# A gated Fourier and window-attention kernel: early loads at its start, another deal of its last projections

## The chip, the cores and the metric

The kernel runs on one core of one Trainium2 chip. The metric is the device time of one execution in microseconds. The engines are called as the profile calls them: PE (TensorE, matrix products) with PEld (its weight loads), DVE (VectorE), ACT (ScalarE), POOL (GpSimd) and SP (SyncE, which issues nearly all transfers here).

## The reference

The input x has 2048 tokens of width 512. Two mixers run on it and a gate mixes them.

```python
x = A_x                                                   # 1 x 2048 x 512
g = sigmoid((x * gate_w).sum(-1, keepdims=True))
# A: Fourier mixing, real part of a transform over width and tokens
a  = einsum("bsd,ed->bse", x, dft_hid_re)
b  = einsum("bsd,ed->bse", x, dft_hid_im)
A  = einsum("ts,bse->bte", dft_seq_re, a) - einsum("ts,bse->bte", dft_seq_im, b)
# B: causal attention in a window of 256 tokens, 32 heads of width 16
q, k, v = split(x @ wqkv)                                 # wqkv: 512 x 1536
scores  = q @ k.T / 4, kept where 0 <= i - j < 256
B       = (softmax(scores) @ v) @ wo                      # wo: 512 x 512
return g * A + (1 - g) * B
```

## The kernel before, in words

Every product of 32-bit data is made of three matmuls on rounded halves (`TERMS`): an operand is split into a rounded part `hi` and a rest `lo` (`split`, lines 76 to 81: a cast, then a subtract on DVE at L81; the cast is on ACT at L78 or on DVE at L80). A 512-column product over 512 inputs is thus 12 matmuls.

There are two strands of work. The attention strand walks over n = 0 to 147: 128 steps of scores (4 head groups times 32 blocks of 64 queries, `s_pair`, L363), and, 19 steps behind (`LAG`), the transposed scores, their exponent and the products with v (`t_pair` L445, `pv` L471). Before a step's scores its heads are laid into zero-padded tiles (`make_pad`, L344 and L346, which multiply by the 0/1 column `half`). Per eight steps (index u) the row maxima and sums are split, turned by PE and copied out (`ml_split`, `ml_turn` at L383, `ml_rows`), and loaded as extra rows of the keys (`m_ring`), so that the transposed scores hold them; the table `TURN` says at which step each of these comes.

The other strand is `dense()`, a generator that gives one matmul at a time: projections to q and k (L277) and to v and the transform over the width (both L300), then the transform over tokens, output block by output block (16 blocks of 128 tokens; 16 chunks of three matmuls for each half, L523). `fill` takes a set number of its matmuls between the steps of attention. When attention is over, the rest of `dense()` runs alone: that is called the tail here.

PE's order is the order of the program text. The other engines and SP's queue are ordered by hand only in the first block of the text; after that a scheduler orders them, held where the text says so: `mark` and `behind` pin instructions of an engine behind the last marked one, and `late` does so for the work that it is given. SP's queue issues in order: a transfer that waits for its data holds those behind it.

Start: the first quarter (block 0) of x transposed is loaded into buffers of the pool `pt`, which holds attention's exponents later and has four buffers. The other three blocks go through the pool `raw`, which has two buffers and also carries wv and the other weights: `load_x` loads two of the four 128-row pieces of a block, `x_job` splits one and asks for the next load.

Rows 96 to 99 of the second pair of padded tiles hold ones and zeros that meet the maxima's rows: `clear_pads` writes ones with GpSimd and multiplies by the column `mrow` on DVE (L214).

Tail: o, the attention's output, is normalised on DVE (L492) and stored in four quarters to `o_scr`. For each block of 128 tokens, `wo_prep` loads it back turned, in pieces of 512 bytes (`fin<-o_scr`), and splits it (ACT L78, DVE L81; tile `os`), and `wo_block` multiplies it by wo in 12 matmuls (L793) and adds its share to a part that lies in `r_scr` (L795). A transform's block goes to `r_scr` by `add_r` (L735), or straight to the output, if the projection of its block is there already (`mixed`). The loop over `tb` makes, between two blocks of the transform (48 matmuls each), all the output projections that were prepared at the block before, 8 of them together; the last block (`c_final`) ends the kernel with its last two chunks apart (L550).

Of the kernel before, what the change touches and what calls it, by code (L numbers as in the profile page):

```python
# [14 lines left out]
P = 128  # L15
# [4 lines left out]
NP = 4  # L20
# [12 lines left out]
def fnet_window_mix(ctx: ExitStack, tc: tile.TileContext, xT, x, wqk, wv, wr, wi, cr, ci, wo, gw, out):  # L33
# [21 lines left out]
    def ld(dst, src):  # L55
        mark("sp", nc.sync.dma_start(dst, src))  # L56

    def f(ap):
        return ap.bitcast(F32)
# [4 lines left out]
    def mark(e, ins):  # L64
        last[e] = ins.ins
# [10 lines left out]
    def split(hi, lo, raw, act=False):  # L76
        if act:
            nc.scalar.copy(hi, raw)  # L78
        else:
            nc.vector.tensor_copy(hi, raw)  # L80
        nc.vector.tensor_sub(lo, raw, f(hi))  # L81

    def split_psum(hi, lo, ps, scale=1.0):
        mark("act", nc.scalar.activation(hi, ps, AF.Copy, scale=scale))
# [7 lines left out]
    def load_raw(src):  # L92
        raw = st.tile([P, 1024], F32, name="raw", bufs=2)
        ld(raw, src)
        return raw
# [29 lines left out]
    XRAW = {}  # L125

    def load_x(ss, j):
        raw = st.tile([P, 1024], F32, name="raw", bufs=2)
        ld(raw.rearrange("p (k s) -> p k s", k=2), xT[ss, 2 * j:2 * j + 2].rearrange("k p s -> p k s"))
        for c in range(2):  # L130
            XRAW[2 * j + c, ss] = raw[:, HALVES[c]]

    def split_x(ss, dks, act=False):
        for dk in dks:
            XT[dk, ss] = big.tile([P, 2, 512], F32R, name="big")
            split(XT[dk, ss][:, 0], XT[dk, ss][:, 1], XRAW.pop((dk, ss)), act)


    def pt_raw():
# [36 lines left out]
    nc.gpsimd.affine_select(ident[:], f(ident[:]), pattern=[[1, P]], compare_op=OP.is_equal, fill=0.0,  # L176
                            base=0, channel_multiplier=-1)

    cols = const.tile([P, 4], F32, name="half")
    half, side = cols[:, :2], cols[:, 2:]  # L180
    mrow = const.tile([P, 2], F32, name="mrow")
    for t, edges in ((half, ((0, 16, 32, 48, 64, 80), (16, 32, 48, 64, 80, 96))), (mrow, ((96, 98), (98, 100)))):
        nc.gpsimd.memset(t, 0.0)
        for h in range(2):
            for i, e in enumerate(edges[h]):
                a = t[:, h:h + 1]
                nc.gpsimd.affine_select(a, a, pattern=[[0, 1]], compare_op=OP.is_ge, fill=1.0 - i % 2,
                                        base=e - 1, channel_multiplier=-1)

    nc.vector.reduce_sum(side[:, 0:1], f(ident[:]).rearrange("p (r h) -> p h r", h=2)[:, 0],  # L190
                         axis=mybir.AxisListType.X)
# [17 lines left out]
    def clear_pads():  # L209
        for t in pads[1]:  # L210
            nc.gpsimd.memset(f(t[96:128]), 1.0)
            for h in range(2):
                a = turned(t)[96:128, :, :, h]
                nc.vector.tensor_scalar(a, f(a), mrow[96:128, h:h + 1], None, op0=OP.mult)  # L214


    gl = const.tile([P, 16], F32, name="gl")
# [301 lines left out]

    def c_part(w, chunks, ab, ps, ends):  # L520
        for i in chunks:
            for n, (a, b) in enumerate(TERMS):
                nc.tensor.matmul(ps, w[a][:, i % 8 * 128:i % 8 * 128 + 128], ab[SC[i]][:, b],  # L523
                                 start=i == ends[0] and a + b == 0, stop=i == ends[1] and a == 1)
                job(i % 8 * 3 + n + 1)
                if i != chunks[-1] or a == 0:
                    yield

    def c_block(get, half, tb, ab, done):
        ps = ps_d.tile([P, 512], F32, name="dc", tag="d")  # L530
        for j in range(2):
            yield from c_part(get((half, tb * 2 + j)), range(16)[8 * j:8 * j + 8], ab, ps, (0, 15))
            if j == 0:
                yield
        ended.append(lambda: late(done, tb, ps))
        yield

    def c_final(get, ab, r):
        ps = ps_d.tile([P, 512], F32, name="dc", tag="d")
        g = g1[:, 15:16]  # L540
        for j in range(2):
            w = get((1, 30 + j))
            yield from c_part(w, range(16)[8 * j:8 * j + 8 - 2 * j], ab, ps, (0, 13))
            yield
        late(nc.vector.scalar_tensor_tensor, r, ps, g, r, OP.mult, OP.add)
        for c, dma in ((slice(0, 256), nc.sync), (slice(256, 512), nc.scalar)):
            ps2 = ps_a.tile([P, 512], F32, name="t", tag="st")
            for i in (14, 15):
                for a, b in TERMS:
                    nc.tensor.matmul(ps2[:, c], w[a][:, i % 8 * 128:i % 8 * 128 + 128], ab[SC[i]][:, b, c],  # L550
                                     start=i == 14 and a + b == 0, stop=i == 15 and a == 1)
            nc.vector.scalar_tensor_tensor(r[:, c], ps2[:, c], g, r[:, c], op0=OP.mult, op1=OP.add)
            dma.dma_start(out[15][:, c], r[:, c])
        yield
# [22 lines left out]
    def late(fn, *args):  # L577
        with behind("act", "dve"):
            return fn(*args)  # L579
# [6 lines left out]
    def dense():  # L586
        warm()
        with behind("sp"):
            wraw = [load_raw(wv[i]) for i in range(2)]
        wvs = [late(split_raw, r, True) for r in wraw]  # L590
        qk_first(wq0)
        load_x(1, 0)
        load_x(1, 1)
        yield
        def x_job(ss, dk):
            late(split_x, ss, (dk,), ss == 1)
            if dk % 2 and ss < 3:
                load_x(ss + 1, dk // 2)

        for ss in range(4):  # L600
            if ss < 3:
# [117 lines left out]
                                  add(lambda t: r_scr[0][t], lambda t: r_scr[2][t]),  # L719
                                  next_b if j else None, tb + 1 if j and tb < 15 else None)  # L720
        ab = nxt
        wait = []

        mixed = {}

        def r_in(tb):
            return r_scr[2 if tb in lasts else 0][tb]
# [15 lines left out]
                                  add(lambda t: r_scr[2][t], lambda t: r_scr[1][t], wait.append),  # L743
                                  None if j else next_b, tb + 1 if tb + 1 < SWITCH else None)
        for tb in range(SWITCH, 16):
            if FIN:
                while ended:
                    ended.pop(0)()
            if tb in O:
                mixed[tb] = wo_block(tb, 0)  # L750
            for w in [w for w in wait if w in O]:
                wait.remove(w)
                ld(out[w], wo_block(w, 1))
            if FIN and tb < 15:
                for w in (tb + 1, *wait[:-(-len(wait) // (15 - tb))]):
                    wo_prep(w)
            yield from c_block(pieces.get, 1, tb, ab, add_r) if tb < 15 else c_final(pieces.get, ab, mixed.pop(15))

    FIN = []

    def attention_done():
        fin = const.tile([P, 8192], F32R, name="fin", tag="ring0")
# [15 lines left out]
    def wo_prep(tb):  # L778
        oraw = ORAW[0]
        ORAW.append(ORAW.pop(0))  # L780
        ld(oraw, o_scr[tb // 4][:, :, tb % 4 * P:tb % 4 * P + P].rearrange("g p t -> p g t"))
        O[tb] = OS[0][:, next(slot) % 8]
        split(O[tb][:, 0], O[tb][:, 1], oraw[:], True)

    def wo_block(tb, half):
        o = O.pop(tb)
        r = ev.tile([P, 512], F32, name="ev")
        ld(r, r_scr[half if half or tb < 16 - SWITCH else 2][tb])
        ps = ps_a.tile([P, 512], F32, name="t", tag="st")
        n = 0  # L790
        for g in range(NG):
            for a, b in TERMS:
                nc.tensor.matmul(ps, o[:, a, g], FIN[0][:, g // 2, g % 2, b], start=n == 0, stop=n == 11)  # L793
                n += 1
        nc.vector.scalar_tensor_tensor(r, ps, g0[:, tb:tb + 1], r, op0=OP.mult, op1=OP.add)  # L795
        return r
# [5 lines left out]
    def need(key):  # L802
        while key not in have:
            next(stream)
# [23 lines left out]
    ctx.enter_context(tc.manual_schedule(engines={mybir.EngineType.PE}))  # L828
    N = NG * NB
    TURN = (8, 1, ml_split), (9, 1, ml_turn), (9, 2, ml_rows), (12, 0, m_ring)  # L830
    need(("qk", 0, 0))
    ring_ahead(0)
    need(("v", 5))
# [10 lines left out]
    for n in range(N + LAG + 1):  # L844
        if n in (1, 3, 5):
            for i in range(2):
                clear_rows(1 - i, (n + 1) // 2)
        if n == 7:
            clear_pads()
        k = n - LAG  # L850
        ring_ahead(n + 1)
        if k in (-1, 4):
            v_spread(0 if k < 0 else 4)
        if k in (-4, -1, 4):
            v_next({-4: 0, -1: 4, 4: 8}[k])
        if n == 0:
            make_pad(0, 0)
        for p in range(NP):
            if n < N:
                s_pair(n, p)  # L860
            fill(n)
            if 0 <= k < N:
                t_pair(k, p)
            if p == 0:
                make_pad(0, n + 1)
                if k >= -1:
                    make_pad(1, k + 1)
            fill(n)
            for at_n, at_p, do in TURN:
                u, j = divmod(n - at_n, 8)  # L870
                if p == at_p and j == 0 and 0 <= u < 16:
                    do(u)
            if p == 3 and k % 8 == 6 and 0 <= k < N:
                l_load(k // 8)
            if p == 0 and full:
                o_out()
            if p == 2 and (k - summed >= (5 if more else 3) or k == N):
                for j in range(summed, k):
                    pv(j)
                summed = k  # L880
            if p == 3 and 4 * spread - 5 < summed and 4 * spread < N and n >= fresh:
                v_spread(4 * spread)
                spread += 1
                v_next(4 * spread)
                fresh = n + 2
# [49 lines left out]
```

## Time and profile before

| | us |
|---|---|
| median of 3 runs | 853.51 (853.19 to 854.07) |
| the profiled execution, time | 854.57 |
| the profiled execution, span | 852.9 |
| PE busy | 844.8 (99%) |
| DVE busy | 615.8 (72%) |
| ACT busy | 593.7 (70%) |
| POOL busy | 251.9 (30%) |
| bytes moved by transfers | 160.99 MB, mean 189 GB/s |

The span runs from the first to the last instruction that the profiler saw; the time of that execution holds a little more around it. In a timeline a row is start, duration, engine, line, operation, output<-inputs, size and count, and in brackets the idle time of the engine before it and what ended that. A `c` in front of a product's name marks the transform over tokens (`dc`), `dqk`, `dv` and `dab` the projections, `s` and `t` the scores and the transposed scores; `t` is also the result of an output projection.

### The profile page before, as it was taken

The numbers are of one execution on the slowest core, as the hardware profiler recorded it, in microseconds if no ns is written. First come the engines' busy times: TensorE is split into PE (matmuls) and PEld (weight loads), VectorE is DVE, ScalarE is ACT, GpSimd is POOL, SyncE is SP. The second block draws the span as 40 slices with busy tenths as digits, with TensorE's granted clock in tenths as the row PEclk, the third lists the DMA queues.
The fourth block names the chain that finished last, engine by engine and source line by source line (L and its number), as shares of the span: only waits on it lengthen the run. The fifth ranks groups of instructions, "written<-read, shape, count | busy, mean of one in ns | idle before, by whom it ended". The sixth has DMA issues, their size and how long they took to land.

```text
span 852.9 us, 16687 instructions
## 1 busy us (share of the span) xinstructions
PE 844.8 (99%) x5166; PEld 691.3 (81%) x5166; DVE 615.8 (72%) x2013; ACT 593.7 (70%) x1793; POOL 251.9 (30%) x585
## 2 busy tenths in 40 slices
PE   9999999999999999999999999999999999999998
PEld 7788788788788888888878887888888887877887
DVE  5588978667878787669777787788888774437531
ACT  5388798878888987779878897778777765532200
POOL 9000222333332333333423324333243354510000
PEclk9999999999999999999999999999999999999999
DMA  7876578576675275444435557989784344359542
GB/s 255 276 235 201 172 247 249 198 236 210 205 249 181 59 210 127 152 125 143 148 120 145 164 144 216 286 278 292 242 225 140 117 153 144 124 176 303 158 147 98
DMA packets 94344, 160.99 MB, mean 189 GB/s; under 512 B 26800, under 2 KB 35760, under 8 KB 94256
## 3 DMA queue, kind: packets, MB, share of 16 engines
q1 hardware_dynamic: 93824, 159.28, 59.8%
q8 instruction: 40, 0.66, 0.3%
q10 hardware_dynamic: 432, 0.66, 0.2%
q14 instruction: 48, 0.39, 0.1%
HBM read 108.27 MB, written 51.64 MB: 187 GB/s over the span
## 4 chain that ended last, share of the span: by engine, by line
PE 92%; DMA 4%; DVE 2%; ACT 1%; issue 1%; SPq 0%; DVEq 0%; ACTq 0%
PE dc L523 39%; PE dab L300 10%; PE s L363 9%; PE t L445 8%; PE o L471 8%; PE dqk L277 8%; PE t L793 5%; PE dv L300 4%; DMA raw<-xT 1%; DMA fin<-o_scr 1%; DMA o_scr<-ev 1%; DVE sm L365 1%; DMA pt<-wqk 0%; DVE big L81 0%; SPq L56 0%
## 5 line engine op out<-in xcount | busy, mean ns | idle before, releaser
L368 ACT ACTIVATE sm<-sm,ml 128x320 f32<-128x320 f32 (+4 forms) x512 | 277.9, 544 | 101.1 <-DVE ml L365 96.4
L523 PE MATMUL dc<-big,hi 128*128 128x512 f32 x1020 | 344.4, 393 | 0.0
L365 DVE CUSTOM_DVE_ANT_0 sm<-s,mask 128x320 f32<-128x320 f32 (+4 forms) x512 | 235.3, 464 | 113.2 <-PE s L363 91.5
L523 PE MATMUL dc<-big,lo 128*128 128x512 f32 x510 | 200.6, 393 | 0.0
L523 PEld LDWEIGHTS dc<-big,hi 128*128 128x128 f32 x1020 | 179.7, 188 | 21.4
L446 ACT ACTIVATE pt<-t 128x320 f32<-128x320 f32 (+4 forms) x392 | 160.3, 411 | 43.0 <-PE t L445 40.9
L450 POOL TENSOR_SCALAR_AFFINE_SELECT pt<-pt 128x128 f32<-128x128 f32 x196 | 72.2, 368 | 302.0 <-ACT pt L446 299.8
L363 PE MATMUL s<-ring,pad 128*128 128x320 f32 (+4 forms) x512 | 157.7, 308 | 0.0
L445 PE MATMUL t<-ring,pad 128*128 128x320 f32 (+4 forms) x512 | 154.1, 301 | 0.1
L346 DVE TENSOR_SCALAR pad<-ring,half 96x256 fp32r<-96x256 f32 x384 | 119.9, 358 | 13.5 <-PE t L445 13.3
L363 PEld LDWEIGHTS s<-ring,pad 128*128 128x128 f32 x512 | 96.1, 188 | 30.3 <-issue 9.0
L445 PEld LDWEIGHTS t<-ring,pad 128*128 128x128 f32 x512 | 96.1, 188 | 22.0 <-DVE ml L365 1.0
L523 PEld LDWEIGHTS dc<-big,lo 128*128 128x128 f32 x510 | 95.9, 188 | 13.8 <-issue 1.6
L368 ACT ACTIVATION_READ_ACCUMULATOR sm<-sm,ml 128x1 f32 x512 | 97.7, 191 | 0.0
L428 POOL TENSOR_SCALAR vpad<-vr,half 128x256 f32<-128x256 f32 x64 | 60.5, 958 | 124.9 <-DMA vr<-v_scr 75.7
L579 DVE TENSOR_TENSOR lo<-raw,hi 128x512 fp32r<-128x512 f32 x142 | 96.8, 691 | 0.1
L300 PE MATMUL dab<-hi,big 128*128 128x512 f32 x256 | 89.2, 394 | 0.0
L277 PE MATMUL dqk<-big,hi 128*128 128x512 f32 x240 | 85.7, 394 | 1.5 <-DVE big L81 0.9
L579 DVE CAST hi<-raw 128x512 fp32r<-128x512 f32 x142 | 60.1, 432 | 18.7 <-PE dc L523 13.0
L344 ACT ACTIVATE pad<-ring,half 96x256 fp32r<-96x256 f32 x128 | 66.6, 520 | 0.0
L454 POOL TENSOR_SCALAR_AFFINE_SELECT pt<-pt 128x128 f32<-128x128 f32 x172 | 62.0, 361 | 0.1
L446 ACT ACTIVATE home<-t 128x320 f32<-128x320 f32 (+4 forms) x120 | 49.0, 408 | 13.4 <-PE t L445 11.5
(97 smaller groups left out, 915.3 us busy)
## 6 DMA issues: line engine op xcount, KB each, us to landing
qk_scr<-home SPq DMA_DIRECT2D x32, 512.0 KB
ring<-qk_scr SPq DMA_DIRECT2D x32, 512.0 KB
raw<-cr SPq DMA_DIRECT2D x32, 512.0 KB
raw<-ci SPq DMA_DIRECT2D x32, 512.0 KB
r_scr<-ev SPq DMA_DIRECT2D x42, 256.0 KB
ev<-r_scr SPq DMA_DIRECT2D x42, 256.0 KB
ab_scr<-home SPq DMA_DIRECT2D x20, 512.0 KB
big<-ab_scr SPq DMA_DIRECT2D x20, 512.0 KB
```

Of the source, the lines that this page charges most:

```text
L277: nc.tensor.matmul(ps, w[a][:, c:c + 128], XT[dk, ss][:, b], start=n == 0, stop=n == 11)
L300: nc.tensor.matmul(ps, XT[dk, ss][:, a, c * 128:(c + 1) * 128], wh[b], start=n == 0, stop=n == 11)
L346: nc.vector.tensor_scalar(dst, src, half[:96, h:h + 1], None, op0=OP.mult)
L363: nc.tensor.matmul(ps[:, :w], PAD[0, n][:, p], ring[1][:, p, k0:k0 + w], start=True, stop=True)
L365: mark("dve", nc.vector.tensor_tensor_reduce(out=sm[:, :w], in0=ps[:, :w], in1=mask[:, WIN - w:], scale=1.0, scalar=3e38, op0=OP.add, op1= ...
L368: mark("act", nc.scalar.activation(sm[:, :w], sm[:, :w], AF.Exp, bias=nm[:, c], scale=-1.0, accum_out=l[:, c]))
L445: nc.tensor.matmul(ps[:, :w], PAD[1, n][:, p], ring[0][:, p, q0:q0 + w], start=True, stop=True)
L446: nc.scalar.activation(pt[:, p, :w], ps[:, :w], AF.Exp, scale=-1.0)
L450: nc.gpsimd.affine_select(a, a, pattern=[[0, 2], [2, 64]], compare_op=OP.is_ge, fill=0.0, base=1, channel_multiplier=-1)
L471: nc.tensor.matmul(OT[g, sb][32 * p:32 * p + 32, q - sb * 512:e - sb * 512], v2[:, p], pt[:, p, q - q0:e - q0], start=first, stop=kb == 8 ...
L523: nc.tensor.matmul(ps, w[a][:, i % 8 * 128:i % 8 * 128 + 128], ab[SC[i]][:, b], start=i == ends[0] and a + b == 0, stop=i == ends[1] and a ...
L579: return fn(*args)
```

## The change

Four things are changed.

1. x's block 1 is loaded into buffers of the pool `pt`, right behind the two loads of wv; block 2 goes to `raw` at the place where block 1 was loaded, and only block 3 is still asked for by `x_job`. The subtract of these splits is marked for DVE, so that marked work follows it.
2. For the first maxima (u = 0) the table `FIRST` takes the place of `TURN`: the turn and the copying of its rows come at step 10, pairs 0 and 1, where they came at step 9, pairs 1 and 2.
3. The pad rows are made by GpSimd alone, by two `affine_select` for each head parity and tile (eight on 32 x 256 in all); `mrow` and the four L214 go.
4. In the tail, `tail_step` runs before every fourth chunk, that is at every 12 matmuls of the transform. It takes up to two output projections that were prepared at least three steps before, and prepares further ones, blocks 15 and 14 first, then those that wait, as long as there are fewer than seven. In the built program, 46 matmuls of the transform follow the last product with v before the first output projection (70 before), and then groups of 24 projection matmuls and 12 of the transform alternate, eight times; 30 of the transform and the last 12 (L550 before) end it. Before it was 70, 96 projection matmuls, 48, 96, 42 and 12. The first group of 24 is blocks 15 and 14.

```diff
     def load_x(ss, j):
-        raw = st.tile([P, 1024], F32, name="raw", bufs=2)
+        raw = pt_raw() if ss == 1 else st.tile([P, 1024], F32, name="raw", bufs=2)
...
-            split(XT[dk, ss][:, 0], XT[dk, ss][:, 1], XRAW.pop((dk, ss)), act)
+            mark("dve", split(XT[dk, ss][:, 0], XT[dk, ss][:, 1], XRAW.pop((dk, ss)), act))
...
             for h in range(2):
                 a = turned(t)[96:128, :, :, h]
-                nc.vector.tensor_scalar(a, f(a), mrow[96:128, h:h + 1], None, op0=OP.mult)
+                for base, sign in ((-2 * h, 1), (2 * h + 1, -1)):
+                    nc.gpsimd.affine_select(a, f(a), pattern=[[0, NP], [0, 64]], compare_op=OP.is_ge, fill=0.0,
+                                            base=base, channel_multiplier=sign)
...
     def c_part(w, chunks, ab, ps, ends):
         for i in chunks:
+            if FIN and i % 4 == 0:
+                tail_step()
...
-    def c_final(get, ab, r):
+    def c_final(get, ab):
...
+        while wait:
+            tail_step()
+        r = mixed.pop(15)
...
             wraw = [load_raw(wv[i]) for i in range(2)]
+            load_x(1, 0)
+            load_x(1, 1)
         wvs = [late(split_raw, r, True) for r in wraw]
         qk_first(wq0)
-        load_x(1, 0)
-        load_x(1, 1)
+        load_x(2, 0)
+        load_x(2, 1)
         yield
         def x_job(ss, dk):
             late(split_x, ss, (dk,), ss == 1)
-            if dk % 2 and ss < 3:
-                load_x(ss + 1, dk // 2)
+            if dk % 2 and ss == 2:
+                load_x(3, dk // 2)
...
         for tb in range(SWITCH, 16):
-            if FIN:
+            now.append(tb)
+            if tb == 15:
                 while ended:
                     ended.pop(0)()
-            if tb in O:
-                mixed[tb] = wo_block(tb, 0)
-            for w in [w for w in wait if w in O]:
-                wait.remove(w)
-                ld(out[w], wo_block(w, 1))
-            if FIN and tb < 15:
-                for w in (tb + 1, *wait[:-(-len(wait) // (15 - tb))]):
-                    wo_prep(w)
...
+    def tail_step():
+        t = next(clock)
+        for tb in [tb for tb in O if born[tb] < t - 2][:2]:
+            if tb in wait:
+                wait.remove(tb)
+                ld(out[tb], wo_block(tb, 1))
+            else:
+                mixed[tb] = wo_block(tb, 0)
+        for tb in (15, 14, *wait):
+            if tb not in O and tb not in mixed and len(O) < 7 and (tb > now[-1] or tb in wait):
+                wo_prep(tb)
+                born[tb] = t
...
     TURN = (8, 1, ml_split), (9, 1, ml_turn), (9, 2, ml_rows), (12, 0, m_ring)
+    FIRST = (8, 1, ml_split), (10, 0, ml_turn), (10, 1, ml_rows), (12, 0, m_ring)
...
-            for at_n, at_p, do in TURN:
+            for at_n, at_p, do in TURN if n > 12 else FIRST:
```

More of the change, by code (lines that the diff above doesn't have):

```diff
@@ L80, in split @@
             nc.vector.tensor_copy(hi, raw)
-        nc.vector.tensor_sub(lo, raw, f(hi))
+        return nc.vector.tensor_sub(lo, raw, f(hi))
     def split_psum(hi, lo, ps, scale=1.0):
@@ L177, in fnet_window_mix @@
                             base=0, channel_multiplier=-1)
[L179 to L188, printed above, removed]
+    cols = const.tile([P, 16], F32, name="half")
+    half, side = cols[:, :2], cols[:, 2:4]
+    nc.gpsimd.memset(half, 0.0)
+    for h in range(2):
+        for i, e in enumerate(range(16 * h, 96 + 16 * h, 16)):
+            a = half[:, h:h + 1]
+            nc.gpsimd.affine_select(a, a, pattern=[[0, 1]], compare_op=OP.is_ge, fill=1.0 - i % 2,
+                                    base=e - 1, channel_multiplier=-1)
     nc.vector.reduce_sum(side[:, 0:1], f(ident[:]).rearrange("p (r h) -> p h r", h=2)[:, 0],
@@ L721, in dense @@
         ab = nxt
-        wait = []
-        mixed = {}
         def r_in(tb):
@@ L745, in dense @@
         for tb in range(SWITCH, 16):
-            if FIN:
+            now.append(tb)
+            if tb == 15:
                 while ended:
                     ended.pop(0)()
-            if tb in O:
-                mixed[tb] = wo_block(tb, 0)
-            for w in [w for w in wait if w in O]:
-                wait.remove(w)
-                ld(out[w], wo_block(w, 1))
-            if FIN and tb < 15:
-                for w in (tb + 1, *wait[:-(-len(wait) // (15 - tb))]):
-                    wo_prep(w)
-            yield from c_block(pieces.get, 1, tb, ab, add_r) if tb < 15 else c_final(pieces.get, ab, mixed.pop(15))
-    FIN = []
+            yield from c_block(pieces.get, 1, tb, ab, add_r) if tb < 15 else c_final(pieces.get, ab)
+    FIN = []
+    now = []
+    wait = []
+    mixed = {}
+    born = {}
+    clock = iter(range(99))
+    def tail_step():
[5 more added lines that the diff above has]
+            else:
+                mixed[tb] = wo_block(tb, 0)
+        for tb in (15, 14, *wait):
+            if tb not in O and tb not in mixed and len(O) < 7 and (tb > now[-1] or tb in wait):
+                wo_prep(tb)
+                born[tb] = t
     def attention_done():
```

## The prediction

> **What bounds the kernel now.** I read the busy shares first, then the chain of waits, then who waits for whom on the matmul engine, then the timelines around the places that the diff touches. In the page, the first line is the share of busy time, the second the granted clock over 40 slices, the third the chain that ended last, by engine.
>
> ```profile
> PE 844.8 (99%) x5166; PEld 691.3 (81%) x5166; DVE 615.8 (72%) x2013; ACT 593.7 (70%) x1793; POOL 251.9 (30%) x585
> PEclk9999999999999999999999999999999999999999
> PE 92%; DMA 4%; DVE 2%; ACT 1%; issue 1%; SPq 0%; DVEq 0%; ACTq 0%
> ```
>
> TensorE is busy for 844.8 us of 852.9 and its instructions are the same in number and kind after the change. So time can come only from TensorE's waits, or be lost to new ones. The view of waits, for PE alone, lists all those of any size: line that waited, releaser, total us, times, longest.
>
> ```profile
> PE dv L584 <- DVE ev L146: 1.5, 1, 1.5
> PE dqk L277 <- DVE big L81: 0.9, 1, 0.9
> PE s L383 <- DVE mlh L377: 0.7, 1, 0.7
> PE dqk L277 <- DVE home L86: 0.6, 1, 0.6
> PE t L793 <- ACT os L78: 0.6, 1, 0.6
> PE s L265 <- DVE big L81: 0.4, 1, 0.4
> ```
>
> These are 4.7 us together. The first and the last belong to the start-up code that the diff leaves alone. Any edit can win only what its own row holds: at most about 1 us each.
>
> **Part 1, x's second block early.** Timelines around 25 us, PE first, then DVE, then two transfers and the issue of wv out of the chain and SP's queue:
>
> ```profile
> 24.76 0.39 PE L277 MATMUL dqk<-big,hi 128*128 128x512 f32 x1
> 26.05 0.50 PE L277 MATMUL dqk<-big,hi 128*128 128x512 f32 x1 [0.91 <-DVE big L81]
> 26.39 0.40 PE L277 MATMUL dqk<-big,lo 128*128 128x512 f32 x1
> ```
> ```profile
> 23.73 0.43 DVE L80 CAST big<-raw 128x512 fp32r<-128x512 f32 x1 [4.42 <-DMA raw<-xT]
> 24.20 0.69 DVE L81 TENSOR_TENSOR big<-raw,big 128x512 fp32r<-128x512 f32 x1
> 25.31 0.69 DVE L81 TENSOR_TENSOR big<-raw,big 128x512 fp32r<-128x512 f32 x1
> ```
> ```profile
> 11.46 3.57 DMA raw<-xT
> 17.42 6.29 DMA raw<-xT
> 4.25 1.69 SPq L56 DMA_DIRECT2D raw<-wv  x2
> ```
>
> DVE runs in its own order. Its last subtract for block 1 (25.31) stands behind the cast of block 2 (23.73), which sat 4.42 us until a load of x landed. TensorE needs that subtract. In steady flow it starts a 512-column matmul every 0.2275 us (the tail's rows below give that: 782.35 − 766.88 over 68 steps). So the wait costs 26.05 − 24.76 − 0.23 = 1.06, and the next start comes at 0.34 in place of 0.23, another 0.11: **1.18 us**, rounding included.
>
> In the changed program block 1 goes into the four idle pt buffers, is issued on SP right behind wv (which ends at 5.94) with its second half once a wq buffer is free, near 10.2, and the four L81 of block 1 stand on DVE ahead of block 2's cast. By the slower of the two transfers shown, 6.29, the second half is there at about 16.5, some 8 us before TensorE wants it. Block 2's loads move up from 17.42 to the two places in SP's queue where block 1's stood (11.46 on), so the first stores of q, k and v issue when they did; but the transfers now run beside those stores, the one thing that this step could harm. The readers of what is stored are the ring loads and then the first pads and scores:
>
> ```profile
> L346 DVE TENSOR_SCALAR pad<-ring,half x18: 343/345/350, 32.8 to 58.4; 96x256 fp32r<-96x256 f32 x18
> L363 PE MATMUL s<-ring,pad x31: 191/287/314, 35.0 to 59.8; 128*128 128x320 f32 x15, 128*128 128x64 f32 x4, 128*128 128x128 f32 x4, 128*128 128x192 f32 x4
> ```
>
> Pads come at 32.8 and scores at 35.0, and TensorE's scores will be wanted 1.18 earlier; a pad of 0.35 leaves about 0.7 us of slack. I take the full −1.18; bounds −1.2 and 0.
>
> **Part 2, pad rows on GpSimd, and the later first maxima.** Four L214 leave DVE and eight selects on 32x256 come to POOL. The nearest price of such a select is L203, 1.23 for two on twice the columns:
>
> ```profile
> 6.25 1.23 POOL L203 TENSOR_SCALAR_AFFINE_SELECT pad<-big 32x512 fp32r<-32x512 f32 x2
> 22.12 0.87 POOL L187 TENSOR_SCALAR_AFFINE_SELECT half<-half 128x1 f32<-128x1 f32 x6
> ```
>
> Eight are at most 4.9 us. If all stood ahead of the last selects on half, which end at 22.99, half would be ready at 27.9, still ahead of the pads at 32.8 that read it: nothing gained or lost. The work removed from DVE stood beside the wait of part 1 and is counted there. FIRST moves the turn of the first maxima (u = 0, near step 9) by half a step up to one pair. The waits on L377 and L86 above lie at n = 17 and later, 93 to 100 us, where TURN holds as before. So zero, with a bound of one wait of that kind, 0.7 us, as a loss; a gain needs a wait at u = 0, and the view has none.
>
> **Part 3, the output projections in the tail.** This is where it is decided. Four views: PE's timeline, the chain of waits, DVE's and SP's timelines.
>
> ```profile
> 766.07 0.54 PE L471 MATMUL o<-pt,vpad 128*32 128x128 f32 x16
> 766.88 0.64 PE L523 MATMUL dc<-big,hi 128*128 128x512 f32 x2
> 782.35 0.39 PE L523 MATMUL dc<-big,lo 128*128 128x512 f32 x1
> 783.33 22.54 PE L793 MATMUL t<-fin,os 128*128 128x512 f32 x96 [0.59 <-ACT os L78]
> ```
> ```profile
> 764.55 4.45 DMA fin<-o_scr
> 771.21 6.50 DMA o_scr<-ev
> 777.73 4.90 DMA fin<-o_scr
> 782.66 0.63 ACT os L78
> ```
> ```profile
> 769.62 0.69 DVE L492 TENSOR_TENSOR ev<-o,ev 128x512 f32<-128x512 f32 x1
> 775.63 0.74 DVE L735 SCALAR_TENSOR_TENSOR ev<-dc,g,ev 128x512 f32<-128x512 f32 x1
> ```
> ```profile
> 770.13 0.43 SPq L56 DMA_DIRECT2D fin<-o_scr  x1
> 772.42 2.94 SPq L56 DMA_DIRECT2D fin<-o_scr  x4
> 776.40 1.22 SPq L56 DMA_DIRECT2D r_scr<-ev  x1
> ```
>
> The last value product ends attention at 766.5. From there the first output projection needs a chain: DVE normalises (769.62), SP stores that quarter of o (6.50 us to landing), SP loads one token block of it back (4.90), ACT rounds it (0.63). It is done at 783.3, and TensorE, which has 70 matmuls of the transform to fill the time, still waits: 783.33 − 782.35 − 0.23 = 0.75 us.
>
> After the change TensorE has only 46 of them there (counted in the built program's order); then come 24 projection matmuls, then 12 more of the transform, and so on. The two blocks that go first are 15 and 14, prepared first, and both lie in that last quarter. The first projection is due at 766.88 + 45 × 0.2275 = 777.12, 24 steps or 5.46 us earlier than before. Does the chain get shorter by as much? Its store loses one fin load ahead of it (770.13) and issues at about 770.7. But the load of block 15 stands on SP behind the r_scr store at 776.40, which waits for L735 on DVE and took 1.22 to issue; that L735 has the same work ahead of it after as before. So the load leaves between 776.8 (an issue of the usual 0.4) and 777.6; I take the middle, 777.3. Its landing takes 4.45 by the row at 764.55 or 4.90 by the row of this very load. How full the transfers are is in the windows (last two columns, share and GB/s):
>
> ```profile
> 774.00:777.00 3.00, 3.00 (x15) 2.49 (x14) 2.91 (x7) 0.87 (x2) 0.00 (x0) 1.00 1.00 362
> 777.00:780.00 3.00, 3.00 (x15) 2.49 (x14) 3.00 (x6) 0.00 (x0) 0.00 (x0) 1.00 1.19 318
> 780.00:783.00 3.00, 2.74 (x13) 1.93 (x11) 0.05 (x1) 0.34 (x1) 0.00 (x0) 1.00 1.12 352
> ```
>
> They are full from 774 on, and the same loads are merely dealt in another order, so I take 4.45, with ends 3.57 (the 11.46 load) and 4.90. Landing 781.75, rounding and its waits 0.65: TensorE starts at 782.4 and has waited **5.3 us** where it waited 0.75: **+4.53**. Ends: 776.8 + 3.57 + 0.65 = 781.0, so a wait of 3.9 and +3.1; and 777.6 + 4.90 + 0.65 = 783.2, so 6.0 and +5.3. All the other waits behind it are covered: blocks 14 and 15 arrive together, and the later ones have 36 matmuls, 8.2 us, for each pair where a load and a rounding take 5.1. The end is the same: 30 chunk matmuls, then the last output.
>
> **The sum.** Against the profiled execution (span 852.9, time 854.57, so 1.67 lie around the span): 852.9 − 1.18 + 4.53 = 856.25, and 857.92 with the 1.67. The median of the runs is 1.06 below the profiled one, so the forecast is 853.51 + 3.35 = **856.9 us**. About 0.2%, 1.7 us here, is what a measurement can tell from no change.
>
> **The rivals.**
>
> *A slow restart.* TensorE's first matmuls ran at half speed:
>
> ```profile
> 1.51 3.78 PE L584 MATMUL dv<-ev 128*128 128x512 f32 x8 [1.51 <-DVE ev L146]
> 5.09 1.49 PE L265 MATMUL s<-big,hi 128*128 128x512 f32 x4
> ```
>
> That is (5.09 − 1.51)/8 = 0.4475 a step against 0.2275, although the clock row above stands at 9 throughout, so eight of them cost 1.8 us. If an idle of 5.3 us brings this back, the time is 858.7. For it: the start. Against it: nothing in this trace shows it later; after the gap of 0.98 at 783.33 the 96 matmuls ran at 0.23, but no wait inside the kernel is longer than 1.3. [...] Chance 0.20.
>
> *The gain at the start is given back.* If TensorE, 1.18 us earlier, only waits longer for DVE at 93 to 100 us (the L377 and L86 rows) or for the first scores, or the early load does not move the subtract up, part 1 is worth nothing: 853.51 + 4.53 = 858.0. For: both rows end on DVE. Against: DVE is 72% busy and sits idle waiting for scores. Chance 0.10.
>
> *The tail loses little.* If the load of block 15 is not held behind the r_scr store and leaves when its data are there, with the quicker transfers: 770.7 + 4.45 + 3.57 + 0.65 = 779.4, a wait of 2.3, +1.5; in all 853.8, the same. For: the transfers are below full between 769 and 774. Against: the queue is in order. Chance 0.13.
>
> *Faster.* Had the store and the load 3.57 each, with nothing held, the projection could start at 778.5, a wait of 1.4 and +0.6; with the waits on L377 and L86 (1.3) also gone, since DVE has less to do, that is −1.18 + 0.6 − 1.3 = −1.9: 851.6. It is decided by whether the data of block 15 are rounded before 778.9, where the tail's loss equals the gain at the start. Against: two full transfers in a row at 774 to 783. Chance 0.06.
>
> **How the numbers follow.** The forecast itself has 0.51 (855.4 to 857.7 by its ends). Slower by over 0.2%: 0.51 + 0.20 + 0.10 = 0.81. Same: 0.13. Faster: 0.06. The range takes in the equal case below (853.8) and, above, the slow restart at 858.7 with 0.5 of the 0.8 by which the tail's upper end exceeds its middle: 853.8 to 859.2.
>
> **What would show it.** Right: no L277 wait near 25 us; one wait on the first projection, on ACT's os and behind it fin<-o_scr, of 4 to 6 us some 46 matmuls after the last value product; every later stretch as before. Wrong: a first projection that waits under 2 us (the chain was shorter than I read it), a wait elsewhere in the tail, or steps of 0.44 after the wait (the slow restart).

## The result and the profile after

The changed kernel takes 860.54 us (median of four runs, 859.52 to 861.38) against 853.35 before: a ratio of 1.0082, 95% interval 1.0065 to 1.0100. The forecast was 856.9 with a range up to 859.2; the sign was right and the size was not. The profiled execution has 861.38, its span 859.6, 6.7 more than before. Two executions among the runs below took 2162 and 3661 us, far above the others of their kernels, and count in no ratio.

The page first: share of busy time, granted clock in 40 slices, chain by engine. TensorE is as busy as before, and one slice of the clock near the end, the 37th (774 to 795 us), is below 9.

```profile
PE 846.5 (98%) x5166; PEld 693.2 (81%) x5166; DVE 615.7 (72%) x2009; ACT 593.1 (69%) x1793; POOL 256.7 (30%) x588
PEclk9999999999999999999999999999999999998999
PE 93%; DMA 3%; DVE 2%; ACT 1%; issue 0%; SPq 0%; ACTq 0%; DVEq 0%
```

The view of waits of the changed kernel, PE alone (line that waited, releaser, total, times, longest):

```profile
PE t L808 <- ACT os L78: 6.3, 1, 6.3
PE dv L589 <- DVE ev L146: 1.5, 1, 1.5
PE dqk L277 <- DVE home L86: 0.8, 1, 0.8
PE s L383 <- DVE mlh L377: 0.6, 1, 0.6
PE dab L300 <- DVE home L88: 0.5, 1, 0.5
```

The wait at 25 us on L81 is gone, the one on the first output projection (L808, which was L793) has grown from 0.6 to 6.3, and one on L300 is new. Where they lie is in PE's timeline, and behind it SP's timeline, both after:

```profile
765.21 0.54 PE L471 MATMUL o<-pt,vpad 128*32 128x128 f32 x16
776.05 0.39 PE L525 MATMUL dc<-big,lo 128*128 128x512 f32 x1
782.73 7.93 PE L808 MATMUL t<-fin,os 128*128 128x512 f32 x24 [6.29 <-ACT os L78]
790.49 0.62 PE L525 MATMUL dc<-big,hi 128*128 128x512 f32 x2
793.23 5.66 PE L808 MATMUL t<-fin,os 128*128 128x512 f32 x24
```
```profile
769.57 0.38 SPq L56 DMA_DIRECT2D o_scr<-ev  x1
770.58 5.66 SPq L56 DMA_DIRECT2D fin<-o_scr  x5
776.33 0.74 SPq L56 DMA_DIRECT2D r_scr<-ev  x1
777.16 1.02 SPq L56 DMA_DIRECT2D fin<-o_scr  x2
```

The last products with v come 0.86 us earlier than before (765.21 against 766.07). That is this execution and not the edits' worth: the deal alone, without any of the start's edits, had them at 765.04, and the start's edits without the deal at 766.07 (both runs below). Then TensorE waits 782.73 − 776.05 − 0.23 = 6.45 us, where it waited 0.75: +5.70. The first 24 projections take 790.49 − 782.73 = 7.76 us; the next 24 have a duration of 5.66 where the first have 7.93: 2.27 more. Stretches of the same trace (PE, PEld, DVE, ACT and POOL busy, then granted clock, transfers' share, GB/s) say why:

```profile
778.00:780.00 2.00, 0.00 (x0) 0.00 (x0) 0.22 (x1) 0.00 (x0) 0.00 (x0) 1.00 1.13 325
780.00:782.00 2.00, 0.00 (x0) 0.00 (x0) 0.00 (x0) 0.00 (x0) 0.00 (x0) 0.62 1.14 348
784.00:786.00 2.00, 2.00 (x6) 1.52 (x6) 1.32 (x4) 0.00 (x0) 0.00 (x0) 0.50 0.93 326
787.00:788.00 1.00, 1.00 (x5) 0.77 (x5) 0.10 (x1) 0.37 (x1) 0.00 (x0) 0.85 0.28 70
788.00:789.00 1.00, 1.00 (x6) 0.82 (x5) 1.00 (x2) 0.75 (x2) 0.00 (x0) 1.00 0.96 340
```

TensorE's granted clock fell to half while it idled (the mean of 0.62 puts the fall at 780.5, 4.0 us after its last matmul ended and 4.4 after that began) and came back at 787.3, 6.8 us later.

From the last value product to the last matmul the trace before has 83.0 us and the trace after 90.6: 7.6 more, less 0.86 at the start, is 6.7, the whole difference of the spans. This stretch of the tail is used below beside the times, since the executions scatter for reasons that lie ahead of it: in the profiled ones (but for that of 3661 us) the last value product starts between 765.4 and 769.9 us, and neither start is regularly the earlier.

### The profile page after: what moved, and what is told of

Same layout as the page of the kernel before. It is cut to its first block, busy times and chain, and to the rows that moved or that the text cites. A ratio compares the mean times of both kernels' runs of the same rounds, so it can differ in the third digit from the quotient of the medians.

```text
span 859.6 us, 16682 instructions
## 1 busy us (share of the span) xinstructions
PE 846.5 (98%) x5166; PEld 693.2 (81%) x5166; DVE 615.7 (72%) x2009; ACT 593.1 (69%) x1793; POOL 256.7 (30%) x588
## 4 chain that ended last, share of the span: by engine, by line
PE 93%; DMA 3%; DVE 2%; ACT 1%; issue 0%; SPq 0%; ACTq 0%; DVEq 0%
PE dc L525 39%; PE dab L300 10%; PE s L363 9%; PE t L445 8%; PE o L471 8%; PE dqk L277 8%; PE t L808 5%; PE dv L300 5%; DMA fin<-o_scr 1%; DMA qk_scr<-home 1%; PE s L265 1%; DMA pt<-wqk 0%; DVE sm L365 0%; SPq L56 0%; ACT sm L368 0%
## 5 line engine op out<-in xcount | busy, mean ns | idle before, releaser
L300 PE MATMUL dab<-hi,big 128*128 128x512 f32 x256 | 89.3, 394 | 0.5 <-DVE home L88 0.5
```

What stands on the lines that cost most here:

```text
L300: nc.tensor.matmul(ps, XT[dk, ss][:, a, c * 128:(c + 1) * 128], wh[b], start=n == 0, stop=n == 11)
```

## The experiments

The medians below stand beside runs of the kernel before on the same chip, whose median was 853.5 to 854.0. "Tail" is the stretch from the last value product to the start of the last matmul, in the profiled execution.

### Halves of the change

**The new deal alone**, on the kernel before (`c_part`, `tail_step`, `c_final` and the loop as changed; all else as before).

> Only the new deal of the output projections, on the kernel before. Theory (the first projections, blocks 15 and 14, wait for the last quarter of attention, and TensorE restarts slowly after that wait): the loss of the whole change without its gain at the start. In the trace after, the last value product comes 0.86 us earlier than before, so 860.54 + 0.86 = 861.4 us, with a wait of 6 to 7 us on the first projection and some ten matmuls at 0.43 us behind it. Rival (the start is slower or shifts the tail so that the chain collides with other transfers): clearly under 860, with a wait of the first projection under 4 us.

Measured: 861.12 us, ratio 1.0074 (1.0050 to 1.0098), tail 90.0, a wait of 5.5 us on the first projection, slow steps behind it. Run again beside the later experiments:

> Only the new deal of the output projections, as in the first experiment, beside the next three for a comparison in time: 861.1 us, 90.0 us from the last value product to the last matmul, a wait near 5.5 us and a clock under 1.00.

860.38 us, ratio 1.0073 (1.0054 to 1.0092), tail 88.5, a wait of 5.0. The loss is the deal's. PE's first projections in the two runs:

```profile
781.61 8.32 PE L806 MATMUL t<-fin,os 128*128 128x512 f32 x24 [5.34 <-ACT os L78]
782.15 7.35 PE L806 MATMUL t<-fin,os 128*128 128x512 f32 x24 [4.82 <-ACT os L78]
```

The same deal thus waits 6.45, 5.50 and 4.98 us in three traces, counted as above, and the first 24 projections are slow each time: 7.8, 8.2 and 7.2 us. The load of block 15 left 11.6, 10.6 and 10.1 us after the last value product, behind the same five loads.

**Everything but the deal.**

> Everything of the change but the deal of the output projections, which is as in the kernel before. Theory: the gain at the start stays and nothing is lost in the tail: 853.35 - 0.86 = 852.5 us, with the wait of 0.75 on the first projection as before. Rival (the gain at the start is given back further on, in new waits on DVE): 853.3 us or more.

Measured: 853.68 us, ratio 0.9990 (0.9975 to 1.0006): no difference that can be told, neither theory excluded. In its trace the 1000th matmul starts 0.6 us earlier than before, but 0.66 us of new waits near 548 us use that up. Its tail has 81.85 us, with no wait at all on the first projection.

### Which blocks go first

```diff
-        for tb in (15, 14, *wait):
+        for tb in (*wait[:5], 15, 14, *wait):
             if tb not in O and tb not in mixed and len(O) < 7 and (tb > now[-1] or tb in wait):
```

> The changed kernel, but five blocks that attention finished long before are prepared and projected ahead of 15 and 14; count and places of the projection matmuls stay. Theory (only the choice of the first blocks is at fault): no wait on a projection and no slow steps: 860.54 less 6.45 of wait, less about 2.0 of slow restart = 852.1 us, which is under the kernel before. Rival (the fine dealing itself costs: shorter groups, projections beside the transform's loads): the wait only moves to a later group, 855 us or more.

Measured: 854.84 us, ratio 1.0001 (0.9985 to 1.0018), tail 81.85. PE's timeline of this run shows no gap: the chunk's matmul at 778.62 is followed after 0.23 us by the projections, and these run at full speed.

```profile
778.62 0.39 PE L525 MATMUL dc<-big,lo 128*128 128x512 f32 x1
778.85 5.66 PE L808 MATMUL t<-fin,os 128*128 128x512 f32 x24
784.35 0.62 PE L525 MATMUL dc<-big,hi 128*128 128x512 f32 x2
```

The tail did what the theory asked: 8.7 us less than after, and as short as the undealt tail of the run above. The time missed the expected 852.1 by 2.7, and the profiled execution shows where: 1.7 us of waits near 548 us, where DVE sits on a load of the transform's matrix, and 0.8 at 117 us. The same line on the start of the kernel before, with nothing else of the change:

> The kernel before with the new deal, early blocks ahead of 15 and 14; start, pads and turns as before. If the first blocks alone are at fault, the loss of 7.3 us is gone with this one line: 853.4 less up to the 1.2 that the tail of the kernel before loses against 81.85 us, so 852.3 to 853.5 us. If the deal costs by itself, 855 us or more.

853.60 us, ratio 0.9992 (0.9980 to 1.0005), tail 81.85. So the one line carries the whole loss, and dealing out as such costs nothing that these runs can tell.

### How far from the last value product

One and two steps later (`born[tb] < t - 2` becomes `t - 3` and `t - 4`).

> The changed kernel, with projections taken one step (12 matmuls of the transform, 2.73 us) later: 58 matmuls instead of 46 follow the last value product. The stretch from the last value product to the last matmul is the measure, since it is free of what happens earlier: 83.0 us before, 90.6 after, 81.85 with early blocks first. Theory (a chain of 17.2 us from the last value product to the first projection): a wait of 6.45 - 2.73 = 3.7 us. If the clock falls only after more idle time than that (in the changed kernel it fell 4.4 us after the last matmul ended), nothing slow follows: 81.85 + 3.7 + 0.4 = 86.0 us in that stretch, 856 in all. [...]

One step: 858.64 us (five runs, 856.55 to 863.74), ratio 1.0054 (1.0037 to 1.0071), tail 88.5. The wait in the profiled execution was 4.0 us, and the clock fell all the same. Stretches of that run:

```profile
784.00:786.00 2.00, 0.00 (x0) 0.00 (x0) 0.00 (x0) 0.00 (x0) 0.00 (x0) 0.94 1.06 308
786.00:788.00 2.00, 0.79 (x2) 0.57 (x3) 0.70 (x2) 1.24 (x2) 0.00 (x0) 0.50 1.00 388
792.00:794.00 2.00, 2.00 (x9) 1.57 (x8) 1.27 (x2) 1.24 (x2) 0.00 (x0) 0.85 0.76 258
```

The last matmul ended at 783.3; by the 0.94 the fall is at 785.8, after 2.4 us, and by the 0.85 the clock is back at 792.6, again 6.8 us later; twelve steps were slow. In one of the five runs the mean clock is 1.000 and the time 856.55, in the others 0.994 to 0.998 and 858.0 to 863.7: the clock did not fall in every execution. Whether the wait of that one was shorter is not on record.

This trace, the slowest of the five, has a second fall. TensorE waits 2.3 us at 118 us (from 117.58 to 120.13), and at 120.2 the clock halves for 3.4 us although work has begun again. The view of waits, then stretches:

```profile
PE dab L300 <- DVE home L88: 2.2, 1, 2.2
118.00:120.00 2.00, 0.00 (x0) 0.00 (x0) 0.62 (x2) 1.25 (x3) 0.00 (x0) 1.00 0.43 165
120.00:122.00 2.00, 1.87 (x13) 0.76 (x17) 0.55 (x4) 2.00 (x8) 0.54 (x2) 0.54 0.59 232
122.00:124.00 2.00, 2.00 (x21) 0.59 (x13) 0.62 (x1) 0.44 (x2) 0.00 (x0) 0.61 0.81 218
```

So a mean clock below 1 does not tell by itself which wait lowered it.

> The changed kernel, with projections taken two steps later: 70 matmuls follow the last value product, as many as in the kernel before, blocks 15 and 14 still first, dealt out as in the change. Theory: a wait of 6.45 - 5.46 = 1.0 us, full clock, 82.9 us from the last value product to the last matmul, 853.5 in all. Rival (the wait is longer because the chain itself grew by the change, for instance through transfers that the new deal puts beside it): a wait of 2 us or more.

Two steps: 854.40 us, ratio 1.0003 (0.9994 to 1.0013), tail 82.2, no wait on the projections, clock 1.00. With 70 matmuls ahead blocks 15 and 14 may go first. The first projection came 16.2 us after the last value product, so the chain was at least 1 us shorter here than the 17.2 of the theory.

### What held the load of block 15

In the changed kernel it issues at 777.16, behind five loads of other blocks and the store to `r_scr`. Here ACT issues it and that of block 14:

```diff
-        ld(oraw, o_scr[tb // 4]...)
+        (nc.scalar.dma_start if tb in (14, 15) else ld)(oraw, o_scr[tb // 4]...)
```

> The changed kernel with the loads of blocks 15 and 14 issued by ACT, whose queue is empty there, in place of SP, where they stand behind five loads of other blocks and the store to r_scr. If SP's order held them, they leave as soon as the stored quarter has landed, 1 to 2 us earlier than 777.16, and the wait falls from 6.45 to about 4.7 us, tail stretch 88.5 us, 858.5 in all. If the landing of the stored quarter held them, nothing changes: 6.4 us, 90.6 and 860.5.

860.70 us, ratio 1.0081 (1.0066 to 1.0096); wait 4.6 us, tail 88.9. The chain of this run:

```profile
770.52 5.88 DMA o_scr<-ev
776.50 4.94 DMA fin<-o_scr
781.46 0.63 ACT os L78
```

The load leaves at once when the store has landed (776.4), 9.75 us after the last value product, where it left after 11.63 in the changed kernel. So SP's order held it: by 1.9 us against that execution, and by 0.8 in this one, where SP gets past its store to `r_scr` only at 777.26. The time did not show the 1.7 us of the tail: this execution waited 1.6 us at 118 us and reached the tail 1.2 us later.

### The price of the slow clock

27 matmuls whose result is overwritten go ahead of the first projection:

```diff
         ps = ps_a.tile([P, 512], F32, name="t", tag="st")
+        if tb == 15:
+            for _ in range(27):
+                nc.tensor.matmul(ps, ident, nxt[0][:, 0], start=True, stop=True)
```

> The changed kernel with 27 extra matmuls of 512 columns, whose result is overwritten, ahead of the first projection: TensorE works through most of the wait of 6.45 us (27 x 0.2275 = 6.1) and is idle for a few tenths. Theory (an idle TensorE drops to half its clock and takes about 4.6 us of work to get it back): the projections start when they did, near 782.7, but at full speed, so 860.54 - 2.0 = 858.5 us and a granted clock of 1.00 throughout. Rival (the slow steps come from the transfers that are full in the same stretch): still about 860.5 us, with slow steps.

PE's timeline of this run, then one stretch of it:

```profile
778.59 6.35 PE L807 MATMUL t<-big,ident 128*128 128x512 f32 x27
784.78 5.87 PE L811 MATMUL t<-fin,os 128*128 128x512 f32 x24
```
```profile
784.00:786.00 2.00, 2.00 (x10) 1.38 (x9) 1.26 (x2) 1.17 (x2) 0.00 (x0) 1.00 1.05 408
```

The clock stays at 1.00, the 24 projections take 5.71 us, and the tail has 88.3 us, 2.3 less than after, through transfers that are as full as they were (share 1.11, 1.14 and 1.05 from 780 to 786 us against 1.14, 1.02 and 0.93). So the slow steps come from idleness, not from the transfers. But the time was 860.68 us, not 858.5: this execution reached its last value product 2.3 us later than the changed kernel's, with 1.3 at 117 us and 0.9 near 549. Repeated on the start of the kernel before, beside the deal without it:

> The kernel before with the new deal and 27 extra matmuls ahead of the first projection, whose result is overwritten. The stretch was 2.3 us shorter with them on the changed kernel, but not the time. If the slow restart costs 2 us of the time too, and other waits of the changed kernel's start hid that, this one takes 858.8 to 859.3 us beside 861.1 for the one without them. If an earlier end of the wait is paid elsewhere, both take the same.

859.70 us against 860.38, lowest 858.36 against 859.81. In its trace block 15 was rounded at 785.82 and its projections started at 786.69, behind the extra matmuls, which thus cost 0.8 of what they saved. The times differ by 0.7 (medians) to 1.5 us (lowest), which with the 0.8 makes 1.5 to 2.3 for the slow clock; the intervals of the two overlap, so the times alone do not prove it. The trace after gives 1.9 (2.27, less 0.39 by which the first 96 projections of the kernel before were slow as well, at full clock: 22.37 against 21.98).

### The start, part by part

**The early load alone.**

> The kernel before with the early load of x's second block alone. Asked: which edit brings the wait of 0.7 to 2.3 us on a product of L300 near 117 us (ACT waits there for a store of q and k), which no kernel with before's start has. If it is the early load (TensorE is up to 1 us earlier and meets a store whose landing does not move), it stands here too, the wait at 25 us is gone, and the 1000th matmul starts 0.3 to 0.7 us earlier than before (187.68). If not, it starts about 1.1 us earlier and 117 us is clean. In time: 852.5 to 853.5 us, hardly to be told from before.

853.01 us, ratio 0.9978 (0.9952 to 1.0003). In its profiled execution the granted clock falls to 0.16 at 251 us, so its trace is read up to 250 us only: the 1000th matmul starts at 186.1 against 187.7, with no wait near 25 or 117 us.

**The pad rows alone.**

> The kernel before with the pad rows made by GpSimd alone. Expected from both theories: nothing, 853.3 to 853.8 us, no wait at 117 us, and the wait near 25 us shorter by at most the one L214 of 0.35 us that stood in it on DVE.

854.31 us, ratio 1.0015 (0.9999 to 1.0031): no gain, perhaps a small loss. And a wait of 0.4 us at 118 us on L300, though neither of the other edits is there. The 1000th matmul starts at 188.2 against 187.7; with the early load, the pads and the early turn together it starts between 187.1 and 190.6 in eight traces, against 186.1 with the early load alone. So the pads seem to take back part or all of what the early load gains, as far as one trace of each alone can say.

**The turn of the first maxima as before** (with early blocks first).

> The kernel with early blocks first, with the table TURN as before for the first maxima too. If FIRST (which moves the stores of the first maxima in SP's queue) brings the wait at 117 us, it is gone here; if the early load brings it, it stays at 0.7 us or more. The waits on L383 at 93 us and L277 at 98 us stay in both cases. Time 852 to 854.8 us.

852.86 us, ratio 0.9998 (0.9989 to 1.0008); the wait at 117 us is there with 1.4 us, those at 92 and 98 too. So `FIRST` does not bring it, nor does the early load alone. In the changed kernel ACT waits there for a store to land; its chain of waits:

```profile
107.59 9.14 DMA qk_scr<-home
116.81 0.61 ACT home L84
```

That wait stands with the pads on GpSimd and the early turn (0.6 to 2.3 us by the start times, in nine traces), and is 0.3 us or less otherwise. What in the pads' move sets it off is open.

**The later turn for all groups** (early blocks first): `FIRST` in place of `TURN if n > 12 else FIRST`.

> Early blocks first, as in the run with early blocks, and the later turn of the maxima (table FIRST) for every group of eight steps and not for the first alone. Theory: the wait of 0.8 us on the turn at n = 17 (the L383 row) goes, as the split on DVE has half a step more: 0.5 to 0.8 us less than with early blocks first alone, up to the step 1000th matmul. Rival: TensorE then only waits longer at the next place that is tied to DVE or to a store (98 and 117 us), and the 1000th matmul starts no earlier than 187.1 us.

852.65 us (851.86 to 853.46), ratio 0.9982 (0.9964 to 1.0000). The waits at 92, 98 and 117 us are gone together; PE's whole view of waits in this run:

```profile
PE dv L589 <- DVE ev L146: 1.5, 1, 1.5
PE t L445 <- ACT sm L368: 0.3, 1, 0.3
PE s L363 <- DVE ml L365: 0.2, 1, 0.2
```

This is the best version measured, ahead of both kernels, by an amount at the edge of what can be told. The later turn alone, on the kernel before:

> The kernel before with the turn of the maxima half a step later for all groups, nothing else. If the later turn alone takes away the waits at 93 to 103 us (L383, L277, L445, together 1.9 us), the 1000th matmul starts at about 186.0 us instead of 187.68 and the time is about 852 us. If it does so only together with the early load, the sum of waits there stays near 2 us and the time at 853.5.

853.74 us, ratio 1.0006 (0.9982 to 1.0030), though its trace, of the fastest execution of ten, has the same clean view at 93 to 118 us and a span of 850.8. And with the deal, without the early load and the pads:

> The kernel before with the new deal, early blocks first, and the turn of the maxima later for all groups; no early load and no pads on GpSimd. With 0.5 to 1.5 us less in the waits at 93 to 103 us and a tail of 81.85 us: 851.5 to 852.8 us. If the early load is needed too for the 852.65 us of the run with the late turn for all, it stays near 853.5.

853.70 us, ratio 0.9995 (0.9982 to 1.0008): not better than before. Its profiled execution, the slowest of twelve, shows what the early load would have spared it; that this makes the whole difference to the 852.65 is not shown, as that run has the pads on GpSimd too. PE's timeline, then two stretches:

```profile
24.74 0.39 PE L277 MATMUL dqk<-big,hi 128*128 128x512 f32 x1
28.14 0.50 PE L277 MATMUL dqk<-big,hi 128*128 128x512 f32 x1 [3.01 <-DVE big L81]
```
```profile
27.00:30.00 3.00, 1.86 (x6) 1.48 (x7) 2.40 (x6) 0.60 (x1) 0.00 (x0) 0.80 1.05 240
30.00:33.00 3.00, 3.00 (x10) 2.38 (x9) 1.26 (x3) 0.00 (x0) 0.00 (x0) 0.63 1.04 388
```

With the start of the kernel before, the wait that the forecast priced at 1.18 varies with the landing of x: 0.27, 0.54, 0.82, 1.07, 1.12, 2.93 and 3.17 us in seven traces and under 0.2 in an eighth (the late turn alone); in the two longest the clock fell there too. The mean clock of the kernel before was 0.998 or less in 11 of its 96 executions beside the experiments, which fits such a fall. No trace with the early load has it.

## Why the prediction was wrong, point by point

- **What bounds the kernel:** right. All that moved is in TensorE's waits, as listed by the view of waits.
- **Part 1, −1.18:** the wait went, as said, but no gain can be told in the time: the start's edits without the deal measured 853.68 beside 853.80 (0.9975 to 1.0006). In the profiled execution 0.86 of it is left at the last value product and 0.6 at the 1000th matmul, but that is a lucky draw, since the traces with these edits reach the last value product between 0.9 us earlier and 3.3 us later than the trace before. So the rival "given back" happened, at 117 us and not at 93 to 100. What I did not see is that one trace shows one draw of the wait at 25 us: between 0.27 and 3.17.
- **Part 2, zero:** near enough in time; on their own the pads gained nothing and perhaps cost half a microsecond, and the later turn of the first maxima could not be told from none.
- **Part 3, +4.53: the mechanism was right, the term smaller than this execution's.** The forecast had the first projection 16.0 us after the last value product (782.4 against 766.4 in the old clock). It came after 17.2, as late as in the kernel before (16.9), although its store issued earlier. The step that failed here is the load of block 15, put between 776.8 and 777.6 and taken at 777.3: it left 11.63 us after the last value product, in the old clock 778.0, outside my two ends, with five loads (5.66 us of SP's queue) ahead of it, where the trace before has four after its store. Then its landing took 4.87, not the 4.45 that I took from a neighbour while its own row of 4.90 was at hand. Together +5.70. But the forecast of 10.9 us for the load lies inside what the same queue gave: with 15 and 14 first and the loads on SP, seven traces have 10.1 to 11.9, and the two runs of the deal alone waited 5.50 and 4.98 where I said 5.3. Why it leaves up to 1.8 us later in one execution than in another is open.
- **The slow restart, given 0.20 and put at nothing in the sum, is the step that failed in every trace:** +1.9 here, and the first 24 projections took 7.2 to 8.2 us in place of 5.5 in all five traces with a wait of 4 us or more. I priced it at 1.8, about right (with 0.4475 a step, which takes in a first one of 0.59; the others are 0.427), and kept it out of the middle because no wait of the trace before was long enough to show it. Where a forecast itself makes a wait longer than any in the trace, the start's half-speed steps, present in the trace, were the nearest row: 0.427 us a step there and 0.427 behind the wait of the trace after. How long a wait it takes is known only as far as the traces go: the clock fell after 2.2 us (at 120 us) and 2.4 us (at 785.8) of idleness in the run one step later, after 4.0 in the trace after, and stayed full in waits up to 1.7.
- **The sum:** −0.86 + 5.70 + 1.9 = 6.7, the measured difference of the two spans; −1.18 + 4.53 was 3.35.
- **A slip:** under "Faster", the tail's loss equals the start's gain when TensorE starts at 777.12 + 0.75 + 1.18 = 779.05, not 778.9. Nothing hangs on it.

## What to carry to other kernels

When work is moved ahead in a hand-written order, follow the data of the very first piece back to the last producer, and count the matmuls that cover that chain; here the choice of a piece whose data are old was worth some 7 us, and the rebalancing itself nothing that these runs can tell. What the scheduler puts ahead of a load in its queue can hold it (the load of block 15 left 11.63 us after the last value product behind SP's other rows, 9.75 when ACT issued it), so look at those rows in the changed program; even with the same rows ahead, it left between 10.1 and 11.9 us after the last value product. A forecast wait on TensorE that is longer than the 1.7 us at which the clock still stayed full here should be priced with a slow restart on top (1.9 us here), and a wait that ends on a transfer is one draw of several (0.27 to 3.17 us at 25 us).

## What the runs showed of the hardware

- In the traces TensorE's clock halved around waits of 2.3 (at 118 us), 2.9 and 3.2 (at 25 us), 4.0, 4.6, 5.0, 5.5 and 6.45 us (on the first projection); it stayed full with waits up to 1.7 (early blocks first, at 548 us), or with other matmuls in their place (1.00 in the stretches of the run with 27 of them). By their mean clock, 0.995 to 0.998, it fell in all 20 executions of the four kernels whose traces wait 4.6 to 6.5 us; the five kernels with the early load and the pads but without such a wait have 0.999 or more in all of their 49 executions that count.
- At half clock it stayed for 6.83 or 3.41 us: 6.83 in the three traces where TensorE was still idle for over 1 us after the fall, 3.41 in the five where work began before the fall.
- At the half clock a 512-column matmul starts every 0.427 us, at full clock every 0.2275, in the same trace.
- The half-speed steps at the kernel's start, 0.427 us in the traces before and after, last until 5.94 us before and 5.65 after. The clock column reads 1.00 there (from 0 to 5 us), since the record of the clock in these two traces has no entry there: its first one, of full clock, stands where the steps end. In the tail the column does show the fall (0.50 from 782 to 787 us after).
- One load of x, issued at the same place of the same start, landed after 6.29 us in one execution (before) and 8.05 in another (the deal and the late turn).
